# State products behind a score group, token quarters of q first, and a split last output tile, in a transformer block on one core

## The chip, the cores and the metric

One core of a Trainium2 chip. The time is the device time of one execution in microseconds (us), given as the median of several executions on the same chip. Five engines matter here, by the names of the profile: TensorE (PE; its weight loads are PEld), VectorE (DVE), ScalarE (ACT), GpSimd (POOL) and SyncE (SP), which in these kernels only issues DMA transfers (every DMA issue on the page is SP's). A ratio of two kernels is the mean time of one kernel's fast runs over that of the other's fast runs of the same rounds, so it is not quite the ratio of the medians quoted beside it.

## The reference, cut to what matters

```python
def _A_ref(x, wq, wk, wv, wo, beta):            # x: 2048 tokens x 1024, 32 heads of 32
    ...                                          # q, k, v: 4 segments of 512 tokens each
    g = _sigmoid(beta).reshape(1, H, 1, 1)
    M = z = 0
    for s in range(4):
        p = _softmax(qs @ ks.T * scale + mask)   # causal inside the segment
        a_dot = p @ vs
        a_mem = (phi(qs) @ M) / (phi(qs) @ z + 1e-06)
        outs.append(g * a_mem + (1.0 - g) * a_dot)
        M = M + phi(ks).T @ vs                   # the "state products" of this text
        z = z + phi(ks).sum
    return concat(outs) @ wo

h  = x + _A_ref(_layernorm(x), ...)              # LayerNorm without scale
h2 = h + swiglu(_layernorm(h), w1, w3, w2)       # 1024 -> 3584 -> 1024
```

## The kernel before: the parts concerned

The kernel describes each operation once, and its own list scheduler orders the operations of all engines before the program is emitted, with a table of tuned offsets (`SHIFT`) that move single operations. Each engine is given its operations as one list in that order; in the trace of the changed kernel, for example, VectorE idles 0.56 us for x2 while the normalization of x0 stands behind it in the list. Attention works in eight halves (four segments, 16 heads each). A half has ten *score groups* (row-tiled: four 32-row matmuls side by side; the first four start within 0.01 us of each other, at 20.76 us), each followed by one exponential of 1.88 us on ScalarE; dense matmuls of the projections and of the SwiGLU fill the time between them. Then come a *column block* (column-tiled matmuls: row sums, then the products with v) and, in the first three segments, the state products:

```python
def finish(self, s, half, at):
    gd = self.queue(4)
    gm = Group([(7,)]) if s < 3 else None        # PSUM bank 7 for the state products
    ...
    column(Both(gd, gm) if gm else gd, ...)      # row sums
    for j in range(4):
        column(...)                              # products with v
    if gm:
        self.memory(s, half, gm)                 # 64 column-tiled matmuls of 33 columns
    ...
```

The first half-segment is special, as TensorE has nothing to do until x has been loaded and normalized:

```python
loads = [x0, x1, wq[:, :, 0:256], x2, x3, wk[:, :, 0:256], rest of wq, rest of wk, wv]
...
work = [(w, i, Group([(5,), (6,), (7,), (4,)], safe=True)) for w in (wq, wk) for i in range(2)]
for c0 in range(0, 512, 128):                    # token quarters of 128
    for w, i, gr in work:                        # two blocks of q and two of k
        self.mms(gr, ... 8 contraction steps of 128 columns ...)
```

The softmax here doesn't subtract the row's maximum and nothing guards it: scores larger than these inputs give would overflow.

Of the kernel before, what the change touches and what calls it, by code (L numbers as in the profile page):

```python
# [8 lines left out]
ALU = mybir.AluOpType  # L9
# [10 lines left out]

SHIFT = {
    0: (113, 0), 1: (-194, 1), 2: (-667, 0), 3: (-97, 0), 4: (-693, -1), 5: (-458, -1),
    6: (-38, 1), 7: (-273, 0), 8: (-32, 0), 9: (1616, 0), 10: (25, 1), 11: (-286, 1),
    12: (172, -1), 13: (-388, 0), 14: (-1163, 0), 15: (1, -1), 16: (-18, 0), 17: (-393, 0),
    18: (-432, 0), 19: (-332, -1), 20: (-726, 0), 21: (-980, 0), 22: (-590, 0), 23: (-337, 0),
    24: (386, 0), 25: (-423, 1), 26: (-992, 0), 27: (170, 1), 28: (-314, 0), 29: (108, -1),
    30: (-213, 0), 31: (-82, 0), 32: (72, 0), 33: (-46, 0), 34: (-61, 0), 35: (-15, 0),
    36: (66, 1), 37: (-122, 0), 38: (73, 0), 39: (75, 0), 40: (240, 1), 41: (790, 0),
    42: (436, -1), 43: (346, 1), 44: (-203, 0), 45: (-52, 1), 46: (280, 0), 47: (-138, 0),
    48: (-1000, 1), 49: (319, 0), 50: (244, 0), 51: (-194, 0), 52: (-341, 0), 53: (114, 1),  # L30
    54: (236, 0), 55: (443, 0), 56: (472, 0), 57: (-181, 0), 58: (202, 0), 59: (0, 1),
    60: (329, 0), 61: (176, 0), 62: (577, 0), 63: (232, 0), 64: (343, -1), 65: (62, -1),
    66: (-1, 0), 67: (-27, 0), 68: (380, -1), 69: (151, -1), 70: (672, 0), 71: (455, 0),
    72: (333, 0), 73: (389, -1), 74: (-231, 0), 75: (-215, 0), 76: (-1180, 1), 77: (-591, 0),
    78: (60, 0), 79: (105, 1), 80: (-645, 0), 81: (822, 0), 82: (720, 0), 83: (-36, 0),
    84: (290, 1), 85: (278, 0), 86: (781, -1), 87: (738, -1), 88: (264, 0), 89: (-38, 0),
    90: (255, 0), 91: (-292, 0), 92: (489, -1), 93: (276, 0), 94: (340, 0), 95: (-320, 0),
    96: (1003, 1), 97: (-984, 1), 98: (300, -1), 99: (545, 0), 100: (105, 1), 101: (-414, -1),
    102: (1239, 1), 103: (310, -1), 104: (-250, 0), 105: (18, -1), 106: (149, -1),
    107: (-967, 0), 108: (-407, -1), 109: (132, 0), 110: (198, 0), 111: (-185, 0),  # L40
    112: (-466, 0), 113: (484, -1), 114: (-58, 1), 115: (-243, -1), 116: (2, 0), 117: (-382, 1),
    118: (246, 0), 119: (-90, -1), 120: (796, 0), 121: (-239, 1), 122: (350, -1), 123: (22, -1),
    124: (-65, 0), 125: (-125, 0), 126: (75, -1), 127: (-802, 0), 128: (-162, -1),
    129: (-459, 0), 130: (609, 1), 131: (439, 0), 132: (287, 0), 133: (725, 0), 134: (-729, 1),
    135: (-763, 1), 136: (-378, 1), 137: (213, 0), 138: (552, 0), 139: (-94, 0), 140: (666, 0),
    141: (-279, -1), 142: (-1607, 0), 143: (103, 0), 144: (1000, 0), 145: (-281, 1),
    146: (-460, 0), 147: (-775, 0), 148: (-161, 0), 149: (-645, 0), 150: (-119, -1),
    151: (-271, -1), 152: (-125, 1), 153: (-757, 0), 154: (-45, 0), 155: (-1064, 1),
    156: (499, -1), 157: (272, -1), 158: (-539, -1), 159: (-398, 0), 160: (-178, 0),
    161: (-32, 0), 162: (-858, -1), 163: (136, 0), 164: (102, 0), 165: (541, 0), 166: (287, 0),  # L50
    167: (526, 1), 168: (-156, 0), 169: (143, 0), 170: (-57, 1), 171: (232, 0), 172: (-293, 0),
    173: (-111, 0), 174: (-244, 0), 175: (-566, 1), 176: (231, -1), 177: (-352, 0),
    178: (-672, 0), 179: (476, 0), 180: (318, -1), 181: (-30, 0), 182: (-1529, -1),
    183: (442, 0), 184: (314, -1), 185: (-580, 0), 186: (683, -1), 187: (261, -1),
    188: (-351, -1), 189: (-262, 0), 190: (-907, 0), 191: (122, 1), 192: (-381, 0),
    193: (-110, 1), 194: (704, 1), 195: (-226, -1), 196: (996, -1), 197: (-511, 1),
    198: (198, -1), 199: (-599, 1), 200: (-399, 1), 201: (519, 0), 202: (-310, -1),
    203: (10, -1), 204: (-305, 0), 205: (-354, 0), 206: (-422, 1), 207: (-148, 0),
    208: (-508, 0), 209: (-551, 0), 210: (377, 1), 211: (-139, 0), 212: (699, 0), 213: (378, 0),
    214: (236, 1), 215: (424, -1), 216: (-195, -1), 217: (-501, -1), 218: (-302, 1),  # L60
    219: (309, 0), 220: (-919, 0), 221: (321, -1), 222: (24, 1), 223: (-98, 0), 224: (619, 1),
    225: (593, 1), 226: (-320, -1), 227: (-779, -1), 228: (351, 0), 229: (327, 0),
    230: (524, 0), 231: (-389, -1), 232: (-574, 1), 233: (-315, 1), 234: (-277, -1),
    235: (469, 0), 236: (-369, 0), 237: (-511, -1), 238: (180, 0), 239: (-88, 0),
    240: (-241, -1), 241: (-5, 0), 242: (602, 1), 243: (304, 0), 244: (-787, 0), 245: (254, -1),
    246: (449, 0), 247: (1135, -1), 248: (-467, 1), 249: (-501, -1), 250: (130, 1),
    251: (-372, 1), 252: (-158, 0), 253: (1119, 0), 254: (-407, 0), 255: (30, 1), 256: (331, 1),
    257: (-413, 1), 258: (-309, 0), 259: (-293, 0), 260: (93, 1), 261: (200, 1), 262: (852, 0),
    263: (156, 0), 264: (168, 1), 265: (-419, 0), 266: (-101, -1), 267: (995, -1),
    268: (-504, 0), 269: (114, -1), 270: (-156, -1), 271: (230, 0), 272: (-118, 1),  # L70
    273: (-324, 0), 274: (313, 0), 275: (484, -1), 276: (408, -1), 277: (416, 0), 278: (127, 0),
    279: (41, 0), 280: (-85, 0), 281: (-440, 1), 282: (192, -1), 283: (-416, 0), 284: (490, -1),
    285: (-173, 0), 286: (73, -1), 287: (113, 0), 288: (162, 0), 289: (-231, 1), 290: (-91, -1),
    291: (-253, -1), 292: (-197, 0), 293: (-507, -1), 294: (98, 0), 295: (136, 0),
    296: (-846, -1), 297: (-281, -1), 298: (756, -1), 299: (605, 0), 300: (-49, -1),
    301: (266, 0), 302: (222, 0), 303: (163, 0), 304: (15, -1), 305: (7, -1), 306: (171, 1),
    307: (-102, 1), 308: (-164, 0), 309: (573, 0), 310: (36, 1), 311: (-391, -1), 312: (122, 0),
    313: (-258, 0), 314: (-377, -1), 315: (234, 0), 316: (-44, -1), 317: (1293, 1),
    318: (458, 0), 319: (-156, -1), 320: (284, 0), 321: (687, -1), 322: (-244, -1),
    323: (296, 0), 324: (-287, 0), 325: (503, -1), 326: (-600, 0), 327: (447, 0), 328: (409, 0),  # L80
    329: (-186, -1), 330: (17, -1), 331: (-46, 0), 332: (-745, -1), 333: (1259, 0),
    334: (1124, 0), 335: (-208, 0), 336: (-187, 0), 337: (-49, 1), 338: (-90, 0),
    339: (-801, 0), 340: (-433, 0), 341: (19, -1), 342: (229, 0), 343: (-749, 0), 344: (109, 0),
    345: (-144, 0), 346: (795, 0), 347: (79, 0), 348: (-554, 0), 349: (83, 0), 350: (-48, 0),
    351: (-26, -1), 352: (-38, -1), 353: (-200, 0), 354: (-529, 0), 355: (596, 1),
    356: (-272, 1), 357: (259, 0), 358: (330, -1), 359: (258, -1), 360: (345, -1),
    361: (444, 0), 362: (129, 0), 363: (915, 0), 364: (36, 1), 365: (280, 1), 366: (-192, 0),
    367: (208, 1), 368: (829, -1), 369: (19, -1), 370: (-310, -1), 371: (-643, 1),
    372: (-300, -1), 373: (109, 0), 374: (-186, -1), 375: (166, 1), 376: (-1088, 0),
    377: (-657, -1), 378: (-150, 0), 379: (36, 1), 380: (-532, -1), 381: (-323, -1),  # L90
    382: (554, 0), 383: (-401, 1), 384: (-833, 0), 385: (-135, -1), 386: (53, 0), 387: (16, 0),
    388: (548, 0), 389: (-612, 0), 390: (-525, 1), 391: (-475, 0), 392: (-658, 0),
    393: (339, 0), 394: (-515, -1), 395: (-70, -1), 396: (-258, -1), 397: (-860, -1),
    398: (47, 1), 399: (-616, 0), 400: (24, 0), 401: (56, 1), 402: (-245, -1), 403: (4, 1),
    404: (-199, 1), 405: (61, 1), 406: (-1407, -1), 407: (987, 0), 408: (544, 0), 409: (-76, 1),
    410: (194, 0), 411: (-100, -1), 412: (525, 0), 413: (-559, 0), 414: (1023, -1),
    415: (699, 1), 416: (498, 0), 417: (-583, 0), 418: (-521, 0), 419: (-287, 0), 420: (858, 0),
    421: (-596, 0), 422: (-482, 1), 423: (-82, 0), 424: (-41, 0), 425: (-14, 0), 426: (8, 0),
# [65 lines left out]
class Graph:  # L164
# [128 lines left out]
    def dma(self, out, in_, cls=5, deps=(), eng="sp"):  # L293
        n = 1
# [280 lines left out]
class Kernel:  # L575
# [273 lines left out]
    def first_tile(self, t):  # L849
# [10 lines left out]
        for b in range(2):  # L860
# [8 lines left out]
            if t == 0 and b:  # L869
                self.warm(1, [self.g.ops[-1]])  # L870
# [508 lines left out]
```

## Time and profile before

| | before |
|---|---|
| median (3 runs) | 896.09 us, 895.78 to 897.34 |
| profiled execution, span | 895.0 us, clock 1.00 |
| TensorE busy | 880.6 us |
| TensorE before continuous work (about) | 10.9 us, of which 1.8 us useful |
| first score group | 20.76 us |
| stop in the sixth group of state products | 1.26 us from start to start |

How to read such a table: TensorE is nearly never free (busy 880.6 of 895.0 us), so a change that removes no matmul can only win some of the gaps, and each gap must be found by its place in time, not by a percentage. The prediction shows those lines. The columns of the timeline are start, length, engine, line, operation, output <- inputs, and in brackets the idle time before and what ended it.

### The profile page before, as it was taken

Reading aid. Unit: us, or ns where it says so; the run is one execution under the profiler, and the core shown is the slowest. Engines: PE = TensorE matmul, PEld = TensorE weight load, DVE = VectorE, ACT = ScalarE, POOL = GpSimd, SP = SyncE. Lnnn points to the kernel's source line nnn. Section 1 sums busy time; section 2 is a strip of 40 time slices with the busy share of each in tenths; the row PEclk is TensorE's granted clock in tenths of the full one; section 3 lists DMA queues with packets and bytes.
Section 4 is the critical chain, followed back from the end, with each engine's and each line's share of the span. In section 5 each row is a group of like instructions: output and inputs, shape, how many; then the busy total and the mean of one; then the engine's idle time right before and its main releaser. Section 6 shows DMA issues by size and latency. Waiting matters only on the chain.

```text
span 895.0 us, 13604 instructions
## 1 busy us (share of the span) xinstructions
PE 880.6 (98%) x5833; PEld 403.4 (45%) x5921; DVE 417.6 (47%) x631; ACT 287.9 (32%) x306; POOL 173.8 (19%) x226
## 2 busy tenths in 40 slices
PE   8999999999999999999999999999999999999998
PEld 5343444444444444444444444444444444444445
DVE  5784848585848485754555311211334333331111
ACT  6767766656565646111111100000111111110000
POOL 2553445353534343100200000000000000000000
PEclk9999999999999999999999999999999999999999
DMA  7899755634541221753475211113223221301110
GB/s 235 227 212 271 187 142 147 187 92 130 165 99 57 72 70 58 225 153 92 120 224 140 85 36 36 30 46 90 64 60 94 71 71 48 95 24 41 40 37 30
DMA packets 146540, 96.32 MB, mean 108 GB/s; under 512 B 45488, under 2 KB 133680, under 8 KB 146480
## 3 DMA queue, kind: packets, MB, share of 16 engines
q1 hardware_dynamic: 146480, 95.45, 38.8%
q8 instruction: 47, 0.77, 0.4%
q14 instruction: 13, 0.11, 0.0%
HBM read 76.55 MB, written 8.39 MB: 95 GB/s over the span
## 4 chain that ended last, share of the span: by engine, by line
PE 97%; issue 1%; DVE 1%; DMA 1%; ACT 0%; SPq 0%; ACTq 0%; DVEq 0%
PE ps L708 89%; PE ps L1107 4%; PE ps L1057 3%; DMA xs<-in_A_x_dram 1%; PE ps L985 0%; PE ps L1184 0%; ACT et L1069 0%; PE ps L1100 0%; DVE t L1260 0%; DVE hm L1265 0%; PE ps L720 0%; SPq L299 0%; DVE R L1163 0%; ACT sg L1257 0%; DVE Nsb L1171 0%
## 5 line engine op out<-in xcount | busy, mean ns | idle before, releaser
L708 PE MATMUL ps<-hnT,w1b 128*128 128x512 bf16 x876 | 218.4, 379 | 1.4 <-issue 0.3
L708 PE MATMUL ps<-hnT,w3b 128*128 128x512 bf16 x873 | 217.4, 379 | 1.5 <-issue 0.5
L1257 ACT ACTIVATE sg<-ps 128x512 bf16<-128x512 f32 x112 | 66.9, 597 | 403.1 <-PE ps L708 403.1
L708 PE MATMUL ps<-w2b,hm 128*128 128x512 bf16 (+1 forms) x907 | 195.3, 372 | 0.9
L1069 ACT ACTIVATE et<-ps 128x2048 bf16<-128x2048 f32 x80 | 150.0, 1875 | 39.3 <-PE ps L1057 38.9
L1260 DVE SCALAR_TENSOR_TENSOR t<-sg,ps 128x512 bf16<-128x512 bf16 x112 | 76.8, 685 | 169.4 <-ACT sg L1257 169.2
L708 PEld LDWEIGHTS ps<-w2b,hm 128*128 128x128 bf16 x924 | 90.4, 98 | 103.2
L708 PEld LDWEIGHTS ps<-hnT,w1b 128*128 128x128 bf16 x896 | 86.5, 98 | 105.5 <-issue 8.2
L708 PEld LDWEIGHTS ps<-hnT,w3b 128*128 128x128 bf16 x896 | 86.5, 98 | 105.4 <-issue 2.9
L1078 POOL TENSOR_SCALAR_AFFINE_SELECT et<-et 128x512 bf16<-128x512 bf16 x96 | 84.0, 881 | 126.2 <-ACT et L1069 126.0
L1265 DVE SCALAR_TENSOR_TENSOR hm<-t,ps 128x512 bf16<-128x512 bf16 x112 | 76.7, 686 | 50.5 <-PE ps L708 47.9
L1289 DVE TENSOR_TENSOR ob<-hr,ps 128x512 bf16<-128x512 bf16 (+1 forms) x33 | 22.1, 671 | 143.0 <-PE ps L708 143.0
L708 PE MATMUL ps<-wo,oT 128*128 128x512 bf16 x249 | 60.7, 380 | 0.6 <-issue 0.3
L708 PE MATMUL ps<-xnT,wp 128*128 128x512 bf16 (+1 forms) x345 | 59.7, 320 | 1.4 <-issue 0.6
L708 PE MATMUL ps<-hnT,wp 128*128 128x512 bf16 x250 | 59.0, 380 | 0.7 <-issue 0.6
L708 PEld LDWEIGHTS ps<-xnT,wp 128*128 128x128 bf16 x352 | 27.7, 98 | 26.9 <-issue 3.6
L708 PEld LDWEIGHTS ps<-wo,oT 128*128 128x128 bf16 x256 | 23.9, 98 | 29.8 <-issue 2.9
L708 PEld LDWEIGHTS ps<-hnT,wp 128*128 128x128 bf16 x256 | 23.6, 98 | 29.8 <-issue 3.8
L1200 POOL TENSOR_TENSOR oT<-Nsb,R 128x512 bf16<-128x512 f32 x23 | 35.8, 1569 | 4.1 <-DVE R L1197 4.1
L1163 DVE STREAM_TRANSPOSE R<-Rc 128x1024 f32<-128x1024 f32 x28 | 33.6, 1222 | 0.1
L1229 DVE TENSOR_TENSOR h<-h,ps 128x512 bf16<-128x512 bf16 x32 | 21.7, 680 | 25.1 <-PE ps L708 24.9
L1057 PE MATMUL ps<-qT,kT 32*128 32x128 bf16 (+3 forms) x512 | 31.7, 301 | 0.0
(82 smaller groups left out, 520.9 us busy)
## 6 DMA issues: line engine op xcount, KB each, us to landing
w1b<-in_B_w_dram SPq DMA_DIRECT2D x28, 512.0 KB, 3.9
w3b<-in_B_w_dram SPq DMA_DIRECT2D x28, 512.0 KB, 3.8
wp<-in_A_wv_dram SPq DMA_DIRECT2D x8, 1024.0 KB, 5.5
wp<-in_A_wq_dram SPq DMA_DIRECT2D x7, 1024.0 KB, 5.9
wp<-in_A_wk_dram SPq DMA_DIRECT2D x7, 1024.0 KB, 5.7
w2b<-in_B_w_dram SPq DMA_DIRECT2D x7, 1024.0 KB, 8.0
xs<-in_A_x_dram SPq DMA_DIRECT2D x16, 256.0 KB, 5.6
h<-in_A_x_dram SPq DMA_DIRECT2D x16, 256.0 KB, 3.7
```

The lines of the kernel that those rows point to most:

```text
L708: return [e.matmul(p[0](gr), p[1], p[2], start=p[3], stop=p[4]) for p in part]
L1057: ins.append(e.matmul(self.bank(gr, j, 512 - 128 * kc, off), k[r, g0 + g, 128 * kc:128 * kc + 128], q[r, g0 + g, 128 * kc:512], start=True ...
L1069: return [e.activation(et[:, :, :], src, AF.Exp, scale=self.scale)]
L1078: self.pool_op(lambda e, v=v, pat=pat: e.affine_select(v, v, pattern=pat, compare_op=ALU.is_ge, fill=0.0, base=0, channel_multiplier=-1), ...
L1107: ins.append(e.matmul(self.ps[32 * i:32 * i + 32, b * 512 + 128 * kc:(b + 1) * 512], lhsT(i, kc, j), at[i, kc][:, j, :], start=kc == 0 and ...
L1163: return self.dve_op(lambda e: e.transpose(out, src), dve_ns(1024), [Rc[:, t, 2 * n:2 * n + 2, :]], [dst], 2)
L1200: self.either(lambda e, out=out, Ns=Ns, R1=R1: e.tensor_tensor(out, Ns, R1, op=ALU.add), 512, 2, [Ns, R1], [out], 2)
L1229: self.g.op("dve", dve_ns(512), lambda e, gr, hs=hs: [e.tensor_tensor(hs, hs, self.bank(gr), op=ALU.add)], reads=[hs], writes=[hs], cls=1, ...
L1257: self.g.op("act", act_ns(512), lambda e, gr, sg=sg: [e.activation(sg, self.bank(gr), AF.Tanh, scale=0.5)], writes=[sg], cls=0, group=gg)
L1260: e.scalar_tensor_tensor(t1, sg, 1.0, self.bank(gr), op0=ALU.add, op1=ALU.mult)], reads=[sg], writes=[t1], cls=0,
L1265: e.scalar_tensor_tensor(dst, t1, 0.5, self.bank(gr), op0=ALU.mult, op1=ALU.mult)], reads=[t1], writes=[dst], cls=0,
L1289: self.g.op("dve", dve_ns(n), lambda e, gr, hs=hs, ob=ob, n=n: [e.tensor_tensor(ob, hs, self.bank(gr, 0, n), op=ALU.add)], reads=[hs], wri ...
```

## The change

Intent: (1) free the column block of the state products by attaching them to the seventh score group of a half, so that the scheduler places them (they "follow a tenancy of scores"); (2) at the start, let all 128-column matmuls be q's, in two halves of the contraction, with loads in an order that suits that (their rows are 1024 bytes long), and take the load-bound first matmuls earlier; (3) end the last output tile in two pieces of 128 columns, for a shorter last addition; (4) tune the offsets again for this program.

```diff
+MEM = 6
 SHIFT = { ... all ~470 tuned offsets replaced ... }

 def attention(self, s, half):
-            self.scores(s, g0, i, parts, at)
+            self.scores(s, g0, i, parts, at, i == MEM and s < 3)
 def scores(...):
+        gm = Group([(7,)]) if state else None
+        add, more = self.products(s, g0 // 4) if state else (None, [])
             ...                                 # the four or eight score matmuls
+            if state:
+                ins += add(e, mem.banks[0])     # the 64 state products, right behind
+        if state:
+            self.memory(s, g0 // 4, gm)
 def finish(...):
-        if gm:
-            self.memory(s, half, gm)

 def ln_stats(...):                              # (cut)
-  the statistics of x2 wait for the first normalization of x0 (deps=self.applied[0])
+  no such dependence; ScalarE takes the statistics of x1 alone (before: x1 and x3)

 def first_half(self):
-        loads = x0, x1, wq[0:256 cols], x2, x3, wk[0:256 cols], wq rest, wk rest, wv
+        loads = x0, x1, x2, wq[chunks 0-3], wq[chunks 4-7], x3, wk, wv
-        work = two blocks of q and two of k, 8 contraction steps each
+        work = four blocks of q, contraction steps 0-3 of all, then 4-7 of all
+        for i in range(4): self.project(0, "k", 0, i, wk)      # k in 512 columns
...
-            cols = [(0, 512), (512, 256), (768, 256)] if t == 15 else ...
+            cols = [(0, 512), (512, 256), (768, 128), (896, 128)] if t == 15 else ...
```

## The prediction

> **What bounds the kernel now.** I read the busy row of the page first, then its chain of waits, then the chain in order of time, then the timeline of the start and of the end.
>
> ```profile
> PE 880.6 (98%) x5833; PEld 403.4 (45%) x5921; DVE 417.6 (47%) x631; ACT 287.9 (32%) x306; POOL 173.8 (19%) x226
> ...
> PE 97%; issue 1%; DVE 1%; DMA 1%; ACT 0%; SPq 0%; ACTq 0%; DVEq 0%
> ```
>
> TensorE is busy 880.6 of 895.0 us and carries 97% of the chain, at a granted clock of 1.00. All that any change can win without removing matmuls is the 14.4 us in which it does nothing, the mode switches and its dummy warm-up matmuls. So I went through the trace matmul by matmul, from start to start. A 512-column matmul takes 216 ns, a 128-column one 56 ns, a 256-column one 109 ns. From 361.8 us to the end there is nothing above these spacings except missing records, so more than half of the program cannot get faster. What is left is three places.
>
> The first is the start (timeline, TensorE, and VectorE in the same stretch):
>
> ```profile
> 6.45 0.63 PE L720 MATMUL ps<-ident,xs 128*128 128x128 bf16 x8 [0.88 <-DVE xs L862]
> 6.92 0.38 PE L708 MATMUL ps<-oT 128*128 128x512 bf16 x1
> 7.70 1.07 PE L708 MATMUL ps<-xnT,wp 128*128 128x128 bf16 x16 [0.41 <-DMA wp<-in_A_wq_dram]
> 10.00 0.72 PE L720 MATMUL ps<-ident,xs 128*128 128x128 bf16 x8 [1.23 <-DVE xs L862]
> ...
> 8.34 1.29 DVE L831 BATCH_NORM_STATS2 lnst<-xs 128x6 f32<-128x512 bf16 x2 [1.05 <-DMA xs<-in_A_x_dram]
> 9.55 0.72 DVE L862 TENSOR_SCALAR xs<-xs,lnst,rstd 128x512 bf16<-128x512 bf16 x2
> ```
>
> The number in brackets is the idle time before the row. After 16 matmuls on the first token tile TensorE waits until 10.00 for the second tile: VectorE took up the statistics of the third tile (8.34, when its load landed) before it applied the second tile's normalization (9.55). From 10.92 on TensorE runs without a gap. By then it has done 16 transposes and 16 matmuls of 128 columns, 32 x 0.056 = 1.8 us of real work. So 10.92 - 1.8 = 9.1 us of the start are lost: that is the number the change must lower.
>
> The second is the state products (L985, 64 column-tiled matmuls of 33 columns, six times), in the chain in order of time:
>
> ```profile
> 55.31 0.52 PE ps L985 x64
> ...
> 269.39 0.34 PE ps L985 x42
> 269.73 1.07 issue
> 270.81 0.32 PE ps L985 x22
> ```
>
> Five of the six take about 0.52 us; the last stops after 42 matmuls for 1.07 us with no engine to blame ("issue" is a wait that the profile shows no releaser for). The third is the end:
>
> ```profile
> 892.44 0.42 DVE L1289 TENSOR_TENSOR ob<-hr,ps 128x256 bf16<-128x256 bf16 x1 [0.89 <-PE ps L708]
> 892.89 0.33 SPq L299 DMA_DIRECT2D out_dram<-ob  x1
> ```
>
> The last matmul is over at 892.4; an addition of 0.42 us, a store that lands 1.66 us after its issue and 0.45 us of closing make up the rest.
>
> [...]
>
> ```profile
> 20.76 0.40 PE L1057 MATMUL ps<-qT,kT 32*128 32x512 bf16 x4
> 21.09 1.25 PE L708 MATMUL ps<-xnT,wp 128*128 128x512 bf16 x5
> ```
>
> Four row-tiled scores run side by side for one stream of 512 columns (213 ns), but the next dense matmul starts 0.33 us after them: 0.115 us is the switch. Going in costs 0.106, column mode to dense about 0.11 (where it looks like 0.33 the first dense matmul's record is missing; its weight load is there). [...] One such packet starts at 268.55 us, before the 1.07 us stop. State products use instructions fastest: 128 in 0.52 us, against 2 in 0.216 us of dense work. [...]
>
> **The change, part by part.** The instruction order of the changed kernel, built but not run, has the same matmuls: 80 score groups, 6 state products, 6 retrieval groups, the same 512-column work; only 28 matmuls of 256 columns become 56 of 128.
>
> *State products.* Before they stand among column-tiled matmuls (four times between two of them, twice as the last), so they pay no switch: 0.52 us. After, each follows the seventh score group of its half: row mode, column mode, dense. An excursion that paid one switch in and one out now pays three: +0.1 us each, 6 x 0.1 = +0.6 us. Against this, the burst is taken out of the long column block and lies between dense matmuls[...]: I give 0.8 that the 1.2 us (1.73 against 0.52) of the sixth product do not come back: -1.0 us. Bank 7 is also held shorter, but no dense matmul waits for a bank in the trace, so that is worth nothing.
>
> *Start.* Loads are now x0, x1, x2, two halves of wq by contraction rows (rows of 1024 bytes instead of 512), x3, wk, wv. 128-column matmuls now cover q alone, all four output blocks, in two halves of the contraction. VectorE's new order is statistics of x0, of x2, then the application of x0: 0.69 + 0.69 + 0.2 us stand in front of it. In before's durations: statistics of x0 until 5.02; x2 (landing estimated at 4.8 us, x1's 4.12 plus the 0.66 us from x2 to x3) until 6.75; x0 applied from 6.78 instead of 5.89; transposes at 7.3 instead of 6.45; ScalarE's copy at 7.8 to 8.4; first 16 matmuls at 8.4 instead of 7.70. But then the next tiles are ready: x2's and x1's applications run on VectorE from 8.5 to 10.0 while TensorE does the 16 matmuls (until 9.3), and transposes and matmuls alternate without a gap. At 8.4 eight transposes (0.45 us) are done: lost are 8.0 us instead of 9.1, -1.1 us. Two deductions: the second half of wq is needed at 9.5 us. Before, 1.57 MB had landed at 9.04 and 2.10 MB at 10.84; it is at 1.84 MB, so 10.0 by interpolation[...]. I take 0.25 us as the mean of the wait. And all four dense banks are held by q when k begins; q's first block ends 0.67 us before the last matmul and needs 0.2 + 0.6 us for its copy: 0.15 us. Sum of the start: -0.7 us.
>
> *End.* The last addition falls from 0.42 to about 0.28 us (128x132 elements took 0.265 to 0.296), the store may land 0.05 sooner (1.66 for 64 KB, 1.70 for 128 KB), 28 more matmuls cost 28 x 2.5 ns = 0.07. Sum: -0.1 us.
>
> *The re-tuned offsets* move dense matmuls between score groups; in the new order 12 or more dense matmuls (2.6 us) still stand between score groups inside a half, against 1.88 us of the exponential plus about 0.6 of latencies, so I count nothing.
>
> Total: -0.7 - 1.0 + 0.6 - 0.1 = -1.2 us; 896.1 - 1.2 = 894.9.
>
> **Rivals.** (1) The start gains nothing: x0's normalization is delayed for x2, and the second half of wq comes at 10 us or later. For it: in the trace the first weight load landed 2 us later than its place in the queue lets one expect (7.66). Then only switches and stop remain: 895.8. (2) A new wait in the first half: state products now need the transposed keys at the seventh score group, and 28 dense matmuls stand before the first one, as if the order had to wait for them. Key transposes land 3.1 to 5.6 us after issue; if the last comes late, TensorE stops there, once or twice, for about 1 us: 896 to 897. Against it: later halves have their keys early. (3) The stop comes back elsewhere[...]: +1.2 on the sum, 896.1. (4) The switch into the products is hidden and the weights are all there at 9.3: 893.5.
>
> **Range and chances.** The parts spread by some 0.5 (start), 0.5 (stop), 0.3 (switches) and 0.5 us (new waits), and the three runs of before spread over 1.6 us. I take 893.1 to 896.6 for 8 in 10. 2% would be 17.9 us, more than all idle time of TensorE: the chance of faster is 0.005, of slower (a lasting wait) 0.005, within 0.99.
>
> **What would show it.** TensorE's busy share stays at 98% or rises; continuous work from about 8.4 us instead of 10.9; first scores about 1 us later than 20.76 (8 more dense matmuls, 1.73 us, stand before them, less the gain of 0.7). Each score group with products should take about 0.95 us to the next dense matmul (0.213 + 0.1 + 0.52 + 0.11), and no L985 group above 1 us. Last addition 0.28 us. I am wrong if the seventh score groups wait for the key transposes, if dense matmuls stop after 22 us for more than 0.3 us, or if the time leaves the range.

The sum stays -0.7 - 1.0 + 0.6 - 0.1 = -1.2 us; of some terms, this is what stands behind them:

- *-1.0 us, the stop.* The page of the kernel before has 47 packets, 0.77 MB in all, of the kind "instruction" on queue 8; "one such packet" is one of these (268.55 to 269.52 us; TensorE stops from 269.73 to 270.81). That the stop had to do with this packet, and that products between dense matmuls would be spared it, was my estimate from this one place and not shown. The term is 0.8 of the 1.2 us.
- *+0.6 us, the switches.* All from the trace of before. A 512-column score group (20.76 us) is followed 0.327 us later by the next dense matmul. Columns cost 0.417 ns each there, by (109.13 - 55.80) / 128 from the spacings of 256 and 128 columns, so 512 columns are 213 ns by this estimate, and 0.114 us is left for the change. From the last dense matmul to a score it is 0.312 us, 0.096 over the dense spacing of 0.216 (the prediction has 0.106). From the last of the 33-column products to the next recorded dense matmul it is 0.344 us where a first dense matmul, 0.226 us, lacks its record: 0.118 is left.
- *-0.1 us, the end.* 2.5 ns for a matmul cut in two is 2 x 55.80 - 109.13 ns, spacings of before.
- *0.25 us in -0.7, wq's second half.* It is half of the 0.5 us between need (9.5) and interpolated landing (10.0). That it could land by 9.3, as rival (4) supposes too, was my guess and nothing in the trace of before shows it.

## More of the kernel before

The gates g come from beta, 64 bytes per partition. Its load is queued with low priority, and four small activations on ScalarE turn it into `gcol`:

```python
self.g.dma(self.beta[:, :], ..., cls=3)
for n in range(4):
    self.act(self.gcol[...], bt, AF.Tanh, act_ns(8), cls=3, scale=0.5)
```

```profile
17.61 0.60 ACT L731 ACTIVATE kT<-ps 128x512 bf16<-128x512 f32 x1 [0.30 <-PE ps L708]
...
19.20 0.88 ACT L683 ACTIVATE gcol<-beta 32x8 f32<-32x8 bf16 x4
```

ScalarE first copies projections out of PSUM (16.7 to 18.2 us) and only later computes the gates from beta. No idle time stands before them: beta, already the last of the first loads, had landed at 18.12 us.

## The result, and the profile after

| | before | after |
|---|---|---|
| median, us | 896.54 (895.78 to 897.72, 6 runs) | 898.03 (896.59 to 899.36, 6 runs) |
| ratio after/before | | 1.0015, 95% interval 1.0002 to 1.0028 |
| mean clock, run by run | 1.000 in all | 1.000 in four, 0.998 in two |
| profiled span | 895.0 us | 896.9 us |

Within 2% as predicted, but 1.5 us slower where 1.2 us faster was predicted, and outside the range. The page of the changed kernel shows nearly the same amount of work (881.0 us busy against 880.6), so most of the 1.9 us between the two spans are idle time:

```profile
PE 881.0 (98%) x5858; PEld 403.7 (45%) x5949; DVE 416.3 (46%) x627; ACT 287.6 (32%) x307; POOL 175.0 (20%) x227
...
PE 96%; issue 1%; DMA 1%; SPq 1%; ACT 1%; DVE 0%; ACTq 0%
```

I went through the trace matmul by matmul again and put the difference into the places of the prediction.

**The start.** Timeline of the changed kernel:

```profile
6.06 0.69 DVE L832 BATCH_NORM_STATS2 lnst<-xs 128x6 f32<-128x512 bf16 x1 [0.56 <-DMA xs<-in_A_x_dram]
8.08 0.63 PE L719 MATMUL ps<-ident,xs 128*128 128x128 bf16 x8 [1.54 <-DVE xs L866]
9.24 1.05 PE L707 MATMUL ps<-xnT,wp 128*128 128x128 bf16 x16 [0.32 <-ACT xnT L730]
...
15.27 2.62 PE L707 MATMUL ps<-xnT,wp 128*128 128x128 bf16 x44
16.57 0.90 ACT L682 ACTIVATE gcol<-beta 32x8 f32<-32x8 bf16 x4 [0.95 <-DMA beta<-in_A_beta_dram]
17.50 1.57 ACT L730 ACTIVATE qT<-ps 128x512 bf16<-128x512 f32 x3
18.45 4.26 PE L707 MATMUL ps<-xnT,wp 128*128 128x512 bf16 x19 [0.56 <-ACT qT L730]
```

VectorE waits 0.56 us for x2, with x0's normalization standing behind it in its list; the first transposes come at 8.08 us (7.3 predicted) and the first 16 matmuls at 9.24 (8.4 predicted). Then work is dense until 17.9 us (15.27 + 2.62). But k's first matmul needs a bank that q holds (TensorE idles 0.56 us before it, until q's copy), q's copy stands behind the four gate activations on ScalarE, and those wait for beta, the last of the first loads here as well (landed at 16.55 us). The chain of waits that ended last, cut to the start of the program, says the same (columns: start, length, what):

```profile
6.76 9.79 DMA beta<-in_A_beta_dram
...
17.27 0.20 ACT gcol L682
...
17.50 0.61 ACT qT L730
```

So k's start hangs on a load of 64 bytes per partition. The first score group is at 22.65 us; 8 more dense matmuls (8 x 0.216 = 1.73 us) stand before it than in the kernel before, so the start is at 22.65 - 1.73 - 20.76 = +0.16 us instead of the predicted -0.7. This is one profile against one.

**The state products.** In the chain: score group, products, then the wait into dense mode:

```profile
46.04 0.33 PE ps L1064 x8
46.37 0.59 PE ps L985 x64
46.96 0.16 issue
47.12 2.54 PE ps L707 x11
```

From score to products 0.327 us, from products to the next recorded dense matmul 0.823, in all six alike. The record of the first dense matmul is missing (its weight load is there, and 0.226 us belong to it, the spacing behind a first dense matmul where both records are there), so a group costs 0.60 us against 0.52 in the column block: +0.08 us each, +0.5 us in all (+0.6 predicted).

**The stops.** The one stop of the kernel before is gone, and two others have come, in column blocks:

```profile
62.19 4.30 PE ps L1119 x120
66.49 1.63 issue
68.11 0.35 PE ps L1119 x8
...
333.40 4.18 PE ps L1119 x119
337.58 0.37 issue
```

From start to start they take 1.95 and 0.70 us, where the neighbours have 0.03: 2.6 us in place of 1.25, so +1.3 us instead of the predicted -1.0.

**The end.**

```profile
893.48 0.29 DVE L1299 TENSOR_TENSOR ob<-hr,ps 128x128 bf16<-128x128 bf16 x1 [0.70 <-PE ps L707]
894.59 0.29 DVE L1299 TENSOR_TENSOR ob<-hr,ps 128x128 bf16<-128x128 bf16 x1 [0.83 <-PE ps L707]
```

The last addition takes 0.29 us instead of 0.42, and from its start to the end of the span 2.28 us pass instead of 2.59: about -0.2 us with the 28 extra matmuls, as predicted. The sum of the four places, +0.16 + 0.5 + 1.3 - 0.2 = +1.8 us, accounts for the 1.9 us.

**Where the stops stand.** "Issue" names no cause, so I counted TensorE's instructions through the program, from its first weight load: each matmul is two (weight load and matmul), each wait that stands alone one. The queue of instruction packets (queue 8) brings 47 packets of 16,384 bytes; the kernel before has 12,040 instructions of TensorE by this count, the changed one 12,104, and 12,040 / 47 = 256.2. So I count in blocks of 256, one to a packet: 47.0 and 47.3 blocks. Remainders in this table are those of the instruction number on division by 256; packet times are from the trace's DMA records. (The expectations below count up to two more.)

| kernel | block entered, us | packet for the next, us | TensorE stands before | remainder | resumes, us | after the packet's end |
|---|---|---|---|---|---|---|
| before | 266.13 | 268.55 to 269.52 | instruction 5311 | 191 | 270.80 | 1.28 us |
| after | 60.30 | 65.25 to 66.72 | instruction 1215 | 191 | 68.11 | 1.40 us |
| after | 331.62 | 335.55 to 336.70 | instruction 6335 | 191 | 337.95 | 1.26 us |

The place of the blocked instruction in its block is the same in all three. In each of the two programs there are 47 places of remainder 191 for 47 packets, and the two stops of the changed kernel are 6335 - 1215 = 5120 = 20 x 256 instructions apart. From here on a block runs from one such place to the next; why the remainder is 191 and not 0 is not shown. The three blocks in question were used up in 3.4, 5.9 and 5.6 us, and their successors' packets started 2.4 to 5 us after they were entered, took 1 to 1.5 us and needed 1.3 to 1.4 us more. A short block alone does not stop TensorE: one of 5.0 us in the changed kernel (entered at 286.4) and one of 3.8 us in the kernel before (132.8) ran through, as their packets had ended 2.3 and 1.4 us before they were used up. Dense work takes 128 x 0.216 = 27.6 us for 256 instructions, a column block some 4.5 us.

### The profile page after: what moved, and what is told of

The parts are those of the page before. It is cut to its first block, busy times and chain, and to the rows that moved or that the text cites. A ratio compares the mean times of both kernels' runs of the same rounds, so it can differ in the third digit from the quotient of the medians.

```text
span 896.9 us, 13664 instructions
## 1 busy us (share of the span) xinstructions
PE 881.0 (98%) x5858; PEld 403.7 (45%) x5949; DVE 416.3 (46%) x627; ACT 287.6 (32%) x307; POOL 175.0 (20%) x227
## 4 chain that ended last, share of the span: by engine, by line
PE 96%; issue 1%; DMA 1%; SPq 1%; ACT 1%; DVE 0%; ACTq 0%
PE ps L707 88%; PE ps L1119 4%; PE ps L1064 3%; DMA beta<-in_A_beta_dram 1%; SPq L298 1%; PE ps L985 0%; PE ps L1194 0%; DVE t L1270 0%; ACT et L1082 0%; ACT sg L1267 0%; PE ps L1112 0%; DVE hm L1275 0%; ACT gcol L682 0%; ACT qT L730 0%; DVE ob L1299 0%
## 5 line engine op out<-in xcount | busy, mean ns | idle before, releaser
L707 PE MATMUL ps<-w2b,hm 128*128 128x512 bf16 (+2 forms) x934 | 195.4, 366 | 0.9
L1299 DVE TENSOR_TENSOR ob<-hr,ps 128x512 bf16<-128x512 bf16 (+2 forms) x34 | 22.3, 655 | 142.8 <-PE ps L707 142.8
```

The source lines that it names most:

```text
L707: return [e.matmul(p[0](gr), p[1], p[2], start=p[3], stop=p[4]) for p in part]
L1299: self.g.op("dve", dve_ns(n), lambda e, gr, hs=hs, ob=ob, n=n: [e.tensor_tensor(ob, hs, self.bank(gr, 0, n), op=ALU.add)], reads=[hs], wri ...
```

## The experiments

The theory at this point: (A) stops belong to block boundaries that fall into column blocks, wherever they are; (B) k's wait is ScalarE standing before beta; (C) x0's normalization stands behind x2's landing. Rivals: the stops are caused by these particular places or by chance; q's copies and banks are too slow in any case; the extra time is something that the page doesn't show. Theory A of the expectations of e1, e2, e3 and e7 is (A). Eleven runs were made, in three calls (e1 to e4; e5 to e8; e9, e10 and e6 again, these three on another chip); each call has its own runs of the kernel before.

| run | median us (range, runs) | ratio to before, 95% | column-block stops in its profiled run, us | k's wait, us | first scores, us | runs with clock under 1.000 |
|---|---|---|---|---|---|---|
| e1 changed kernel again | 899.72 (898.69 to 901.58, 5) | 1.0035 [1.0023, 1.0047] | 2.5 in three | 2.44 | 25.18 | 5 of 5 |
| e2 + 47 dummies | 897.43 (896.48 to 901.25, 6) | 1.0013 [0.9997, 1.0029] | none | 0.95 | 22.70 | 3 of 6 |
| e3 before + 18 dummies | 899.05 (897.94 to 900.12, 5) | 1.0023 [1.0011, 1.0035] | 3.0 in two (see text) | none | 19.70 | 0 of 5 |
| e4 x0 normalized sooner | 898.41 (896.29 to 900.55, 5) | 1.0021 [1.0009, 1.0034] | 0.7 in one | 1.12 | 22.25 | 1 of 5 |
| e5 beta early | 898.9 (897.48 to 900.54, 6) | 1.0024 [1.0011, 1.0037] | 1.7 in two | none | 23.95 | 5 of 6 |
| e6 all three | 895.65 (895.36 to 896.97, 5) | 0.9989 [0.9978, 1.0001] | none | none | 21.53 | 0 of 5 |
| e7 + 121 dummies | 901.3 (899.92 to 901.53, 5) | 1.0044 [1.0032, 1.0056] | 2.4 in two | 1.32 | 23.96 | 0 of 5 |
| e8 end as before | 898.08 (896.51 to 899.3, 4) | 1.0013 [1.0, 1.0026] | 1.8 in two | none | 24.00 | 2 of 4 |
| e9 e6 without dummies | 898.13 (896.25 to 899.29, 6) | 1.0014 [1.0, 1.0027] | 1.9 in three | none | 21.53 | 1 of 6 |
| e10 e5 + longer warm-up | 899.01 (898.01 to 899.88, 5) | 1.0024 [1.0012, 1.0036] | 1.4 in two | none | 22.42 | 0 of 5 |
| e6 again | 895.56 (895.04 to 897.52, 6) | 0.9991 [0.9978, 1.0004] | none | none | 22.04 | 0 of 6 |

Medians of before in the three calls: 896.62, 896.78 and 896.34 us, 11 runs each, clock 1.000. A stop's length here is from start to start less the spacing of its neighbours.

### e1: the changed kernel once more

No edit. 

> The changed kernel, unedited, a second time. Its first trace has two stops of TensorE inside column blocks, 1.8 us before the last 8 matmuls of the first column block and 0.7 us before the last 9 of the seventh; counted through the program, both fall on the same place of a 256-instruction block as the one stop of the kernel before (instruction numbers 1216, 6337 and 5313: remainders 192, 193, 193). Theory A[...]: stops, if any, stand at instructions with that remainder and nowhere else, each ending about 1.3 us after the end of the fetch packet; their lengths may differ from the first trace. Theory B (a data dependence in the new order): stops at the same two places with the same length, whatever the fetch. Time 897.5 to 898.5 us.

It was slower still, with a clock of 0.996 to 0.998 in all five runs. In the profiled run beta landed at 17.39 us, k's wait grew to 2.44 us, and TensorE came back at half its rate:

```profile
17.42 0.90 ACT L682 ACTIVATE gcol<-beta 32x8 f32<-32x8 bf16 x4 [2.77 <-DMA beta<-in_A_beta_dram]
18.34 1.57 ACT L730 ACTIVATE qT<-ps 128x512 bf16<-128x512 f32 x3
19.36 0.63 PE L707 MATMUL ps<-xnT,wp 128*128 128x512 bf16 x1 [2.44 <-ACT qT L730]
```

The next eight matmuls of 512 columns start 427 ns apart instead of 216: 8 x 0.211 = 1.7 us lost behind the wait. So this wait of 2.44 us cost 1.7 us more than its length, and the clock is one reason why the time of the changed kernel moves by some us from run to run (in e2, below, 896.6 us on average at 1.000 and 899.6 at 0.998). The stops stood at remainder 191 again, all three, two at the places of the first profile with other lengths, one at a new place (385.0 us). The time itself lies above the expected 897.5 to 898.5.

The trace's clock record tells more than the mean. In e1, e5 and e8 it has one stretch at half clock, of 3.41 us each (19.22 to 22.63, 9.29 to 12.70 and 9.10 to 12.51 us). Half a clock over 3.41 us is 0.002 of 897 us, so by this estimate a mean of 0.998 is one such stretch and 0.996 two. In these three profiles the fall lies within 0.9 us of the end of an idle time of TensorE: 2.44 us until 19.36 in e1, 2.15 us until 8.43 in e5, 2.49 us until 8.67 in e8. In e7 an idle time of 2.25 us (6.39 to 8.64) was followed by 16 matmuls in 1.05 us, and the clock held. So the length of an idle time does not alone tell whether the clock falls; what else does is not shown.

That the wait follows beta can be read across the runs: in the five profiles in which k waits, its first matmul starts 1.90 to 1.97 us after beta lands, while beta lands anywhere from 16.15 to 17.87 us.

### e2 and e7: 47 and 121 small dummy matmuls in the idle start; e3: 18 in the kernel before

```diff
 def warm(self, n, deps=()):                     # the warm-up matmuls on zeros
+        if n > 1 and PHASE:                     # PHASE = 47 (e2), 121 (e7), 18 (e3)
+            # behind the warm-up, on the same zeros and the same bank:
+            for k in range(PHASE):
+                e.matmul(ps[32*j : 32*j+32, 33 columns], w[:, 0:32], w[:, 0:33],
+                         start=True, stop=True, tile_position=(0, 32 * (k % 4)))
```

The dummies' results are never read. They lie where TensorE is idle, and each moves all later block boundaries by two instructions. I worked out the spans of the blocks anew for each number of dummies, from the profile of the changed kernel: with none the shortest are 5.0, 5.5 and 5.9 us, with 47 no block after the start is shorter than 8.6 us, with 121 four last 4.1 to 4.8 us.

> The changed kernel with 47 tiny dummy matmuls (94 instructions, about 0.4 us) behind the warm-up, where TensorE idles from 5.9 to 8.05 us; every engine's order is otherwise the same. They move all block boundaries by 94 instructions, so that the shortest time between two boundaries, taken from the first trace without its stops, rises from 5.0 to 8.6 us. Theory A: no stop in any column block, and 1.5 to 2.5 us less than the changed kernel: about 896.0 us. Theory B (data dependence): the stops stay, same time as the changed kernel within 0.3 us.

> The changed kernel with 121 dummy matmuls in TensorE's idle start; nothing else changed. They put several 256-instruction blocks wholly into column blocks (shortest blocks by the trace of the changed kernel: 4.1, 4.1, 4.7, 4.8 us). Theory A[...]: more stops than in the changed kernel, two to four with a sum above 2.5 us, each at remainder 191 to 194 of 256 with the 242 added instructions counted; about 899 to 900. Rival B (the stops belong to the places in the program, or are chance): stops at the changed kernel's old places or none, 898 or less.

> The kernel before with 18 of the same dummy matmuls behind its warm-up (36 instructions; TensorE idles there from 5.57 to 6.42 us). The six shortest times between block boundaries go from 3.4, 3.8, 4.2, 6.2, 6.9, 7.7 to 3.3, 3.5, 3.8, 4.4, 5.2, 5.7 us. Theory A: the stop inside the sixth state product goes from where it is, stops stand at other instructions (remainder 192 or 193 with the 36 added), and as more blocks are short their sum is rather larger, 1 to 4 us: 896 to 899 us. Theory B: the stop stays where it is and the time stays within 0.3 us.

With 47 dummies no column block stopped; the blocks that stopped before now run through (chain of waits of that run, both places):

```profile
62.24 4.46 PE ps L1137 x128
66.70 0.16 issue
...
331.95 4.35 PE ps L1137 x128
336.30 0.16 issue
```

The start remained as it was, with k's wait and the clock: the three runs at full clock took 896.48, 896.5 and 896.94 us (mean 896.6), the three at 0.998 took 897.92, 899.58 and 901.25 us (mean 899.6). So removing the stops alone brought the changed kernel level with the one before (896.62 us) in the three runs in which the clock held.

With 121 dummies the time rose to 901.3 us. In its profiled run, the fastest of the five, I found a long stop (2.21 us from start to start, at instruction 1471 or remainder 191, just before the column block's last matmuls), a short one of 0.3 us (339.5 us, remainder 191), and k's wait of 1.32 us on beta again:

```profile
63.50 4.46 PE ps L1137 x127
67.96 1.99 issue
69.95 0.22 PE ps L1137
```

Two to four stops with a sum above 2.5 us were expected; two of 2.4 us in all came, and two further blocks of 4.7 and 4.8 us ran through. The direction and the place in the block were right. In the kernel before, 18 dummies cost 2.4 us. A new stop of 1.39 us came before a score group, some 2 us behind a column block, at remainder 191, and the stop in the sixth state products stayed, but 18 matmuls earlier in the program's own order:

```profile
96.52 1.32 issue
97.84 0.40 PE ps L1075 x4
...
269.73 0.14 PE ps L1003 x24
269.87 1.48 issue
271.35 0.46 PE ps L1003 x39
```

Before it stopped after 42 of the 64 products, now after 24 (42 - 18). A stop that belonged to a place, a buffer or an engine would not move by exactly the number of dummies. So (A) stands: the stops follow the count of instructions. In all thirteen profiles together there are 19 stops of 0.39 us or more at remainder 191 of score groups, state products and column blocks, and each ended 1.24 to 1.58 us after the end of a packet. The packets also follow the count: with 121 dummies the program crosses 48 such places instead of 47, and the trace has 48 packets. That the packets are what TensorE waits for is still not shown by an experiment, as I cannot make a packet come sooner.

### e4: x0 normalized between x2's two statistics

```diff
+        n = self.g.named                        # after scheduling; all else frozen
+        self.g.move(n["eps", 0], n["stats", 2, 1])
+        for b in range(2):
+            self.g.move(n["apply", 0, b], n["stats", 2, 0])
```

> The changed kernel with three VectorE instructions moved: the eps addition of the first token tile stands before the third tile's statistics, and its two normalizations between the third tile's two statistics; every other order is the same. In the changed trace VectorE waited 0.56 us for the third tile's load with the first tile unfinished, and the first transposes stood at 8.05 us. If that order is what delays the start: first transposes at 7.2 to 7.4 us, first 16 real matmuls at 8.3 to 8.5 instead of 9.24 (then bound by the first half of wq, which landed at 8.24), dense work of q over 0.4 to 0.75 us earlier. Rival: the weight halves bound it anyway, second half at 9.67 us: no more than 0.2 us gained by the first scores (22.65). Column stops as in the changed kernel.

```profile
6.63 0.63 PE L728 MATMUL ps<-ident,xs 128*128 128x128 bf16 x8 [0.95 <-DVE xs L876]
7.92 1.07 PE L716 MATMUL ps<-xnT,wp 128*128 128x128 bf16 x16 [0.44 <-DMA wp<-in_A_wq_dram]
...
16.18 0.90 ACT L691 ACTIVATE gcol<-beta 32x8 f32<-32x8 bf16 x4 [1.51 <-DMA beta<-in_A_beta_dram]
18.05 1.67 PE L716 MATMUL ps<-xnT,wp 128*128 128x512 bf16 x7 [1.12 <-ACT qT L739]
```

Against the first profile, transposes came 1.45 us earlier (6.63 instead of 8.08), the first 16 matmuls 1.3 us earlier (now bound by the first half of wq), and q was finished about 0.9 us earlier. But x2 landed at 5.03 us here and at 6.04 there, so most of this is the load and not the edit, which leaves one of x2's two statistics in front of x0. In e1, without the edit, x2 landed at 5.02: there the transposes came at 7.11, the first 16 matmuls at 8.28, and q ended at the same time as here. So in this pair the edit moved the transposes by 0.5 us and the end of q by nothing. What (C) says is better seen over all profiles: in the seven of the changed kernel's programs with the old order, transposes start 2.04 to 2.09 us after x2 lands (5.02 to 6.63 us); in e6, e9 and e6 again, which have this edit, 1.17 to 1.24 us after it lands. k started only 0.4 us earlier than in the first profile, since beta lands when it lands: q's earlier end turned into a longer wait (1.12 instead of 0.56 us). With one bound at the start lifted, the next one gives most of it back.

### e5: beta's load directly behind x3

```diff
+        q = self.g.order["sp"]                  # the DMA queue's order, all else frozen
+        self.g.move(self.g.named["beta"], q[6])
```

> The changed kernel with one edit: the small load of beta goes directly behind x3 on the DMA queue instead of last; every engine's order is frozen otherwise. Theory A (k's first matmul waits because ScalarE, in order, sits before beta's activations until beta lands at 16.5 us and so copies q late): beta lands by about 11 us, ScalarE's four activations on beta are over before the last matmul of q (by about 13 to 16.5 us), k's wait falls from 0.5 (2.35 and 1.09 in the other runs) to at most 0.25 us, no matmuls at half rate behind it, and the mean clock is 1.000 in nearly all runs where the changed kernel showed 0.996 to 0.998 in some: about 1 us or more under the changed kernel, 896.5 to 897.5, with the stops of TensorE inside column blocks unchanged in kind (0.6 to 2.5 us in all). Rival B (the wait is for q's four copies and banks in any case, beta is incidental): k still waits 0.5 us or more and the time stays at about 898. Rival C (wk lands later as beta is before it): k waits for wk.

Theory B is right about the wait: beta landed at 10.71 us, the gate activations ran without idle time before them, and k followed q without a gap. (This run alone would not show it, as q ended late, at 19.5 us, and e8 has no wait either with beta late; in e10, e6 and e9, with beta early and q ended by 17.1 to 18.0 us, k has no wait.) It was wrong about the clock and so about the time. Five of six runs were at 0.996 or 0.998 all the same, and the profiled run shows where:

```profile
8.43 0.63 PE L728 MATMUL ps<-ident,xs 128*128 128x128 bf16 x8 [2.15 <-DVE xs L875]
8.89 0.38 PE L716 MATMUL ps<-oT 128*128 128x512 bf16 x1
9.59 1.86 PE L716 MATMUL ps<-xnT,wp 128*128 128x128 bf16 x16 [0.31 <-ACT xnT L739]
...
13.51 0.67 PE L716 MATMUL ps<-xnT,wp 128*128 128x128 bf16 x9
```

Sixteen matmuls take 1.86 us instead of 1.05, one every 107 ns. x2 landed at 6.39 us here (6.04 in the first profile of the changed kernel, 5.0 to 6.6 us over all runs with its load order), and TensorE idled 2.15 us between the end of its warm-up and the first transposes. A second place of the lower clock, which I had not suspected: it is wait (C), paid twice.

### e10: e5 with four more warm-up matmuls

```diff
 def warm(self, n, deps=()):
+        if n > 1:                               # behind the warm-up, to shorten the idle time
+            for k in range(4):
+                e.matmul(self.bank(gr), self.oT[0][:, 4, 0:128], w, start=True, stop=True)
```

> The version with beta's load early alone (898.9 us; clock below 1.000 in five of six runs; in its profiled run some thirty 128-column matmuls behind the first transposes took 107 ns instead of 56), with four more 512-column dummy matmuls at the end of the warm-up, which fill 0.9 to 1.7 us of the idle time before the first transposes. Theory (the clock falls because TensorE idles for over 2 us between the warm-up and the first transposes, as x0's normalization waits for x2): the clock is 1.000 in nearly all runs and no matmul of the first 20 us takes twice its time: 1 to 2 us less than before the dummies, 896.8 to 897.8, with the stops inside column blocks still there. Rival (the clock falls for another reason, as after the k wait or by chance): clocks of 0.998 in most runs again, 898.5 or more.

The clock did what the theory said: 1.000 in five of five runs, where e5 had one in six, and no matmul at half rate before 20 us. In its profiled run TensorE idled 1.73 us before the first transposes, against 2.15 us in e5's. But e5 ran in another call and on another chip, and e5 itself was not repeated beside e10, so a difference of the chips is not excluded. The time did not follow: 899.01 us. In the profiled run, the slowest of the five, two waits that e5's did not have took the gain, besides two stops in column blocks. Both are loads on the DMA queue, not instructions:

```profile
351.29 6.50 DMA h<-in_A_x_dram
357.78 0.05 issue
357.83 2.76 PE ps L716 x12
```

The weights of the output projection's first matmul carry a wait on the semaphore of this reload of x. In the kernel before it had landed 1.7 us before that matmul; in the changed kernel and nearly all its variants it lands 0.04 to 0.5 us before it. Eleven of the thirteen profiles have a landing time of 3.8 to 4.8 us for it, e9 and e10 have 6.6 and 6.5, and there TensorE stood for 1.5 and 1.4 us. At 620 us a load of w3 cost e10 another 0.7 us in the same manner; a variant of the kernel before, e3, waits 0.3 us for the same load, so that one is not new. That the reload of x has lost its slack in the re-tuned order is plain from the times; why it was slow in these two runs I cannot say.

### e6: all three edits; e9: the same without the dummies

Both are the edits of e4 and e5 together; e6 has e2's 47 dummies on top. Apart from the dummies the two programs are the same.

> The changed kernel with all three edits: 47 small dummy matmuls during the start (they shift every later boundary of 256 instructions), x0's normalization ahead on VectorE, beta's load early. If the three causes add: no stop inside a column block (as in the run with the 47 dummies alone), first dense work at about 7.9 us, k's wait at most 0.25 us, first score group at about 21.2 us (22.65 in the changed kernel), clock 1.000: 894.0 to 895.7 us, below both kernels. If the time is ruled by something else (a rival), it stays at 896.5 to 898.

> The version with all three edits once more, on this call's chip: 895.3 to 896.3, clock 1.000 in all runs, no stop inside a column block, and about 1 us below the kernel before of the same call (0.9978 to 1.0001 of it in the call before).

> The version with all three edits, without the 47 dummy matmuls: the changed kernel with x0's normalization ahead and beta's load early, so with the changed kernel's own places of the 256-instruction boundaries. Theory: the start is that of the version with all three (k's wait at most 0.25 us, first score group near 21.3 us, clock 1.000 in all or nearly all runs) and the stops come back, at remainders 191 to 194, 0.6 to 2.5 us in all: 896.2 to 898, about 1.3 us above the version with the dummies of this call. Rival: the dummies helped by keeping the clock up or by chance, and the two are equal within 0.3 us.

```profile
8.27 1.05 PE L719 MATMUL ps<-xnT,wp 128*128 128x128 bf16 x16 [0.56 <-ACT xnT L742]
...
14.66 6.94 PE L719 MATMUL ps<-xnT,wp 128*128 128x128 bf16 x63
14.91 0.89 ACT L694 ACTIVATE gcol<-beta 32x8 f32<-32x8 bf16 x4
...
16.20 1.71 ACT L742 ACTIVATE qT<-ps 128x512 bf16<-128x512 f32 x3 [0.41 <-PE ps L719]
```

That is the start of e6 as the change had meant it: no idle time before the gates, and TensorE's row runs from 14.66 us across the step from q to k. First scores at 21.53 us (22.04 in the other call); less the 1.73 us of extra work that is 19.80 and 20.31, where the old start had 20.76 in its profile but 19.70 in e3, as its first wq columns landed at 7.66 us in the one and 6.47 in the other. So the mended start is as good as the old one; that it is better, these few profiles do not show. No column block stopped (in e6's first profile TensorE waits 0.3 us for a load of wv at 85.0 us, as e2's has 0.2 us, and nothing else of note), and the clock was 1.000 in all eleven runs of both calls. The median is 895.65 us and, on another call, 895.56: 2.4 us under the changed kernel's first result (898.03, in another call), and 0.8 to 1.1 us under the kernel before of the same call. Each of the two intervals against before (0.9978 to 1.0001 and 0.9978 to 1.0004) just includes no difference; that it is really faster than before is likely from two agreeing calls, not proven by either.

Without the dummies the start is as good (21.53 us) and five of six clocks are 1.000, but the median is 898.13 us against 895.56 in the same call: 2.6 us, where 1.3 were expected. Its profiled run, 897.2 us, has three stops in column blocks with 1.9 us in sum and the late reload of x with 1.5 us; e6's profiled run of that call, 893.7 us, has neither, and 1.9 + 1.5 = 3.4 us is nearly all that lies between them. So the dummies do not help by keeping the clock up (it was up in e9, and in e7, where more dummies made it worse), but by where they put the boundaries.

### e8: the end in one piece of 256 columns

```diff
-            cols = [(0, 512), (512, 256), (768, 128), (896, 128)] if t == 15 else ...
+            cols = [(0, 512), (512, 256), (768, 256)] if t == 15 else ...
```

> The changed kernel with its last output tile ended by one piece of 256 columns, as before. Theory: the last addition goes back from 0.29 to 0.42 us, the last store's 64 KB become 128 KB, and from the start of the last addition to the end of the span it is 2.6 us again instead of 2.3; total +0.2 us, which the scatter of the runs hides. Rival: the two pieces are worth nothing (both stores run one after the other), 2.3 us either way.

```profile
895.06 0.42 DVE L1299 TENSOR_TENSOR ob<-hr,ps 128x256 bf16<-128x256 bf16 x1 [0.89 <-PE ps L707]
```

The last addition is back at 0.42 us, and from its start to the end of the span it is 2.51 us against 2.28: 0.23 us, less the 0.07 us that the 28 extra matmuls cost. The medians (898.08 and 898.03) cannot show it. Its profiled run gives a check on B by accident: x2 landed at 6.63 us, TensorE idled 2.49 us and went to half rate (16 matmuls in 1.87 us), so q was finished late, beta was there first, and k did not wait at all.

## Why the prediction was wrong, by its own steps

**What bounds the kernel.** Right: the same three places hold all that moved. TensorE's busy share stayed at 98%.

**Start, -0.7 us: this is one of the two terms that failed. It measured +0.16 us in the first profile and +2.7 us in e1's (25.18 - 1.73 - 20.76).** Its steps failed as follows. The order of VectorE was seen and counted, but with x2 landing at an estimated 4.8 us; it landed at 6.04 (5.0 to 6.6 over the runs), so the transposes came at 8.08 and not at 7.3. The deduction of 0.15 us for k on q's banks measured 0.56 to 2.44 us in five of the six profiles with beta last (in e8, where q ended late, nothing): I had reckoned with the copies' own time and not looked at what stands ahead of them in ScalarE's list. It could be read beforehand, as the order of the built kernel has the gate activations ahead of q's copies, and beta is the last of the first loads in both kernels. And half-rate matmuls after idle times of 2.44, 2.15 and 2.49 us (1.5 to 1.7 us lost in e1, e5 and e8) were in no term. The 0.25 us for wq's second half did not come: it landed at 9.67, before it was needed. Last, the 9.1 lost us that the change was to lower came from one profile; in e3 the same start was 1.06 us earlier, so even a start without these waits had little to win.

**Stop in the sixth state products, -1.0 us: the other term that failed; it measured +1.3 us.** That the stop had to do with a packet of queue 8 was my estimate, and the experiments bear it out as far as its place goes (remainder 191 in all 19 stops, each over 1.24 to 1.58 us after the end of a packet). The step that failed is "0.8 that they do not come back": I looked at the one place that the change thinned out and not at the blocks of the new program. The column block without its state products still takes 128 matmuls in 4.3 us, and the program now has 28 more matmuls and another order, which put boundaries into it. This was rival (3), named with +1.2 us on the sum; the runs in this order showed 0.7 to 2.6 us (e2 and e6 excepted, whose dummies moved the boundaries).

**Switches, +0.6 us:** measured +0.5, in all six products alike. **End, -0.1 us:** measured -0.2. **Offsets, nothing:** not quite. No exponential was late, but reloads that had 1.7 us of slack have 0.04 to 0.5 us now, and in two profiled runs of variants the reload of x cost 1.4 to 1.5 us.

**Rivals.** (1), the start gains nothing, is what was measured, for a reason that it gave (x0 delayed for x2) and for one that it did not (beta). (2), seventh score groups waiting for key transposes, did not happen: from score to products it is 0.327 us six times out of six. (3) happened. (4) did not: the switch out of the products is paid. Two of these sums do not come out of their own terms: (1) gives 896.1 - 1.0 + 0.6 - 0.1 = 895.6 and not 895.8, and (4), 0.6 and 0.25 us below 894.9, gives 894.05 and not 893.5. Nothing rests on either.

**Range.** Two terms of four had the wrong sign, and both were given a scatter of only 0.5 us. The spread of the changed kernel itself, 896.6 to 901.6 us, is larger than the whole range; the wait of 2.44 us in e1, with 3.41 us at half clock at its end, is part of the reason.

What stays open: what makes some packets start up to 4.3 us before their boundary is crossed and others up to 5.2 us after it (both in the changed kernel's first profile), what besides the length of an idle time decides whether the clock falls (it fell after 2.15 us in e5 and held after 2.25 us in e7), and what made the reload of x slow in e9 and e10.

## What to carry to other kernels

When a change reorders the engines, follow each in-order list up to the operation that the next stage waits for, and ask of everything ahead of it what *it* waits for: here four tiny activations on a load of 64 bytes per partition held up the first matmul of k by 0.56 to 2.44 us, and no busy share shows it. A stop that the profile gives to "issue" and that stands at the same remainder of 256 instructions (191 here) can move with the program instead of going away; count it over the new program, and shift the program by a few idle-time instructions to test it. Tuned offsets fit one program: after a change that adds instructions, check again the boundaries, the slack of loads that land just in time, and the idle times behind which the clock fell (2.15 to 2.49 us here).
